# K ahead of q in the load queue, shifted copies behind the keys' copy, and the third w1 in halves of the model dimension

## The chip, the cores and the metric

The kernel runs on one core of one Trainium2 chip. The metric is the device time of one execution in microseconds, as the median of the runs shown. Times inside an execution are counted in microseconds from the start of its profiled span.

## What is computed

Sliding-window causal attention over 8 elements, 8 heads, 576 positions and a head dimension of 64, with a window of 64, followed by a mixture of experts in which a whole element goes to one expert: the mean over positions picks it.

```python
scores = scale * np.matmul(q, k.transpose(0, 1, 3, 2))
mask = (rel >= 0) & (rel < 64)
attn = softmax(np.where(mask, scores, -1e9))
x = matmul(attn, v)            # heads side by side: (8, 576, 512)
...
logits = x.mean(axis=1) @ w_gate                 # 8 experts
e_idx = np.argmax(logits, axis=1)
h = np.maximum(x[mask] @ w1[e], 0.0)             # 512 -> 1024
out[mask] = gate_w[mask, None, None] * (h @ w2[e])   # 1024 -> 512
```

## The kernel before

The attention is cut into 16 units, two for each element: unit u holds four heads of element u // 2. In the tables that a reader sees in the trace, a unit does the following.

- Two DMAs on POOL's queue bring its q and its K from float32 in memory to bfloat16 in SBUF (`load_qk`, tiles `qn` and `kn`, L211 and L214), q first.
- TensorE transposes K and q (`transpose_qk`, 18 small matmuls each, L334, tile `tp`), and a copy on DVE or ACT takes each from PSUM to SBUF (`leave_qk`, tile `dst`, L347, L301, L303).
- The scores come in three blocks (`scores_mm`, L380, tile `sp`). For each, ACT takes the Exp (`scores_out`, L398, tile `pt`) and DVE multiplies with a 0/1 mask (`mask_out`, L405).
- The values are multiplied in two halves of 20 matmuls (`values`, L426, tile `op`); the last third of each half reads the third block of `pt`. DVE divides by the row sums (`norm`, L440 and L442). The values lie in SBUF twice: `va`, cast from float32 by DVE (`cast_part` "whole", L303), and `vb`, the same shifted by 64 rows, which two copies make ("low" and "high", L303, from `va` to `vb`).

After two units an element's x is transposed (`transpose_x`, L463 on PE and L471 on ACT), the gate is computed (`gate`, L507 to L522), and the number of the chosen expert is read into a register of POOL, which then issues the loads of its weights: w1 (`load_w1`, L557 or L561) and w2 (`load_w2`, L567). They go through POOL's one queue, in the order of the program, with the loads of q and K. The expert's work is a stream of chunks (`expert_chunks`): eight chunks of the up projection, 8 matmuls each (`expert_up`, L599, tile `php`, followed by a Relu on ACT at L605 into `hT`), and five of the down projection (`expert_down`, L626 and L635, tile `pso`, followed by a copy into `ob` on DVE or ACT and a DMA on SP's queue).

The main loop runs in steps, from t = 4 on, one per unit. In step t stand the three score blocks and the two value halves of unit t, the transposes of unit t + 1, K's ahead of the first value half and q's between the halves, and `experts(pace)`, which is called eight times in most steps and puts chunks of an earlier element between the parts until an account of units of work is used up. An even step also holds the gate of element t // 2 - 1. The order of the code is the order on each engine (`P` keeps it). Step 6 holds the gate of element 2, the third one, so its chunks run from step 7 on.

PSUM has four buffers (pool `psum`), given out in turn, so a matmul that starts a new tile waits until the tile four places before has been read by ACT or DVE.

Weights come in two forms. For elements 0 to 2, w1 is loaded in pieces of the hidden dimension (`PARTS`; for element 2 two pieces of 512 columns, 512 KB each in SBUF), with the 128 columns of x that meet it side by side; each of the four rows of a piece in a partition is 1 KB long in SBUF. From element 3 on it comes in halves of the model dimension, also 512 KB each, in which a partition's part is one row of 4 KB, and x's columns are then taken with a stride of 2. A chunk needs one piece, but both halves. Elements 3 and 7 start with a pair of chunks (`expert_pair`), which takes the first half for two chunks and then the second half for both:

```python
for kbs in ((0, 1), (2, 3)):
    for f in (ft, ft + 1):
        expert_up(b, f, kbs)
```

Of the kernel before, what the change touches and what calls it, by code (L numbers as in the profile page):

```python
# [156 lines left out]
def kernel(  # L157
# [10 lines left out]
    nc = tc.nc  # L168
    B, H, S, D = q.shape
# [4 lines left out]
    FB = F // 128  # L174
# [5 lines left out]
    def P(ins):  # L180
        tc.keep_in_program_order(ins)
        return ins
# [16 lines left out]
    qv = q.rearrange("b h s d -> (b h s d)").rearrange(  # L199
        "(u s r c) -> u r s c", u=NU, s=2, c=NT * D)  # L200
# [7 lines left out]
    def load_qk(u):  # L208
        qn = qkn.tile([128, 2, NT * D], BF16, tag="qn")
        kn = qkn.tile([128, 2, NT * D], BF16, tag="kn")  # L210
        P(nc.gpsimd.dma_start(out=qn, in_=qv[u]))  # L211
        if u == 0:
            load_v(0)
        P(nc.gpsimd.dma_start(out=kn, in_=kv[u]))  # L214
        qk_tiles[u] = (qn, kn)

    v_tiles = {}

    def load_v(b, behind=None):
        vn = vpool.tile([128, NM, D], FP32, tag="vn")  # L220
        if behind is None:

            P(nc.gpsimd.memset(vn[:, 0, 0:1], 0.0))
        else:

            P(nc.gpsimd.tensor_copy(out=vn[:, 0, 0:1], in_=behind))
        v_tiles[b] = vn
        P(nc.sync.dma_start(out=vn, in_=vv[b]))
# [8 lines left out]
    wg = const.tile([128, KB, E], FP32)  # L237
    P(nc.scalar.dma_start(out=wg.rearrange("p (g kl) e -> p g kl e", kl=2), in_=moe_w_gate.rearrange("(g p kl) e -> p g kl e", p=128, kl=2)))

    wg0 = const.tile([128, KB, E], FP32)  # L240
# [25 lines left out]
    for (half, e, own) in ((0, 0, True), (1, 0, False), (0, 1, False), (1, 1, True)):  # L266
        sl = par[64 * half:64 * half + 64, e, :]
        if own:

            P(nc.gpsimd.affine_select(  # L270
                out=sl, in_=sl, compare_op=ALU.is_ge, fill=OUT, base=0,
                pattern=[[1, 64]], channel_multiplier=-1))
        else:

            P(nc.gpsimd.affine_select(
                out=sl, in_=sl, compare_op=ALU.is_ge, fill=OUT, base=-1,
                pattern=[[-1, 64]], channel_multiplier=1))
    outside = const.tile([128, 3, 6, 64], BF16)
    for c in range(3):
        P(nc.vector.tensor_copy(  # L280
            out=outside[:, c].rearrange("p (g e) w -> p g e w", e=2),
# [165 lines left out]

    def x_chunk(b, kb):

        if b < 3:  # L450
            return slice(128 * kb, 128 * kb + 128)
        return slice(256 * (kb // 2) + kb % 2, 256 * (kb // 2 + 1), 2)

# [31 lines left out]

    def gate_parts(b, kb):

        rows = wg0 if b < 3 else wg
        if kb == 0:
            gparts[b] = small.tile([128, E], FP32, tag="gpart", name=f"gpart{b}")  # L490
            P(nc.vector.tensor_scalar(
                out=gparts[b], in0=rows[:, kb, :], scalar1=pooled[:, b, kb:kb + 1],
                scalar2=None, op0=ALU.mult))
        else:
            P(nc.vector.scalar_tensor_tensor(  # L495
                out=gparts[b], in0=rows[:, kb, :], scalar=pooled[:, b, kb:kb + 1],
                in1=gparts[b], op0=ALU.mult, op1=ALU.add))
# [34 lines left out]
    def gate_weight(b):  # L532
# [8 lines left out]


    PARTS = (((0, 256), (256, 256), (512, 512)),
             ((0, 512), (512, 512)),
             ((0, 512), (512, 512)))

    def w1_part(b, i):
# [2 lines left out]
            :, KB * lo:KB * (lo + n)].rearrange("p (k f) -> p k f", k=KB)  # L550

    def load_w1(b):
        if b < 3:

            src = w1c[experts_of[b]].squeeze(0)
            for i, (lo, n) in enumerate(PARTS[b]):
                P(nc.gpsimd.dma_start(out=w1_part(b, i), in_=src[:, :, lo:lo + n]))  # L557
        else:

            for g in range(KB // 2):  # L560
                P(nc.gpsimd.dma_start(  # L561
                    out=weights[b][0][:, 2 * g:2 * g + 2, :],
                    in_=w1e[experts_of[b]].squeeze(0)[:, g]))
# [17 lines left out]
    def expert_up(b, ft, kbs=(0, 1, 2, 3)):  # L581
        if b == 0:
            part = min(ft // 2, 2)
            at = 256 * (ft // 2) - PARTS[b][part][0]
            w1t, cols = w1_part(b, part), slice(at + ft % 2, at + 256, 2)
        elif b < 3:
            w1t, cols = w1_part(b, ft // 4), slice(ft % 4, 512, 4)
        else:
            w1t, cols = weights[b][0], slice(512 * (ft // 4) + ft % 4, 512 * (ft // 4 + 1), 4)
        xT = xt_tiles[b]  # L590
        if ft == 0:
            h_tiles[b] = hpool.tile([128, FB, S], FP16, tag="hT", name=f"hT{b}")
        hT = h_tiles[b]
        if kbs[0] == 0:
            up_ps[b, ft] = psum.tile([128, 2, 512], FP32, tag="ps", name="php")
        php = up_ps[b, ft]
        for kb in kbs:
            for sc in range(2):
                P(nc.tensor.matmul(  # L599
                    out=php[:, sc, 0:288], lhsT=w1t[:, kb, cols],  # L600
                    rhs=xT[:, kb, ts(sc, 288)],
                    start=(kb == 0), stop=(kb == KB - 1)))
        if kbs[-1] < KB - 1:
            return
        P(nc.scalar.activation(  # L605
            out=hT[:, ft].rearrange("p (sc s) -> p sc s", sc=2),
            in_=php[:, :, 0:288], func=AF.Relu, scale=gatew[:, b:b + 1]))
# [63 lines left out]

    def expert_chunks():
        for b in range(B):
            if b in (3, B - 1):

                yield (lambda b=b: expert_pair(b, 0)), 2.0, nc.vector
            for ft in range(2 if b in (3, B - 1) else 0, FB):
                yield (lambda b=b, ft=ft: expert_up(b, ft)), 1.0, nc.vector
            left = [0, 1, 2, 3]
            tail[0] = True  # L680
            while left:

                if tail[0] and (halves[0] or len(left) == (3 if b == B - 1 else 1)):
                    tail[0] = False
                    yield (lambda b=b: expert_down(b, 4)), 0.9, nc.scalar
                else:
                    mt = left.pop(0)
                    yield (lambda b=b, mt=mt: expert_down(b, mt)), 1.7, nc.scalar
# [134 lines left out]
    for t in range(START + 1, NU + LAG):  # L823
        pace = per_step / 8.0 * 0.96
        on, prev, ahead = t < NU, START + 1 < t <= NU, t + 1 < NU

        def next_gate():
            b = t // 2 - 1
            gate(b, sp_ps[t, 2] if easy and on else None)
            load_w1(b)  # L830
            if START + 5 < t < NU - 3:
                load_qk(t + 3)
            load_w2(b)
            if t in (START + 3, START + 5):
                load_qk(t + 3)
            if t // 2 + 2 < B:
                load_v(t // 2 + 2)
            if t == START + 1:
                load_qk(7)

        gated = START < t <= NU and t % 2 == 0


        easy = gated and t > START + 3
        if t % 2 == 1 and t + 3 < NU:
            load_qk(t + 3)
        if prev:
            transpose_x(t - 1)
        if ahead and t > 5 and not gated:
            cast_part(t + 1, "whole")  # L850
        if on:
            scores(t, 0, easy or not gated)
            scores(t, 1, easy or not gated)
        if t > START + 1:
            experts(pace)
        if easy:
            experts(pace)
            if on:
                scores_mm(t, 2)
        if gated:  # L860

            next_gate()
            if on and not easy:
                mask_out(t, 0)
                mask_out(t, 1)
        if t == START + 1:
            experts(pace)
        if t == NU:
            gate_weight(B - 1)
            okc = row_check()  # L870
        if ahead and t > 5:
            if gated:
                cast_part(t + 1, "whole")
        if not easy:
            experts(pace)
        if on:
            if not easy:
                scores_mm(t, 2)
            scores_out(t, 2)
        if gated and on:  # L880
            gate_weight(t // 2 - 1)
        shifted = ahead and t > 5
        if shifted and not easy:
            cast_part(t + 1, "low")
            cast_part(t + 1, "high")
        if t == START + 1:
            cast_v(t)
        experts(pace)
        if shifted and easy:

            cast_part(t + 1, "low")
            cast_part(t + 1, "high")
        experts(pace)

        if ahead:
            transpose_qk(t + 1, 1, leave=False)
            leave_qk(t + 1, 1, free[0])

        late = t == START + 1
        if late:  # L900
            transpose_qk(t + 1, 0)
        elif on:
            values(t, 0)
        halves[0] = on
        experts(pace)
        experts(pace)
        if ahead and not late:
            transpose_qk(t + 1, 0)
        if late:
            values(t, 0)  # L910
        if on:
            values(t, 1)
        halves[0] = on
        if t == START + 2:
            cast_v(t + 1)
        if t == NU:
            row_flag(okc)
        experts(pace)
        experts(pace)
        if late:  # L920

            cast_v(t + 1)
# [38 lines left out]
```

## Time and profile before

| what | value |
|---|---|
| median of three runs | 216.69 us (215.91 to 217.36) |
| the profiled execution | 216.99 us |
| its span, first to last instruction | 215.1 us |
| TensorE busy | 200.3 us, 93% of the span |
| ACT, DVE busy | 134.8 us, 126.2 us |
| DMA | 45.64 MB moved, 212 GB/s in the mean |

Engines are named as in the profile: PE is TensorE's matmuls, PEld its weight loads, DVE VectorE, ACT ScalarE, POOL GpSimd and SP SyncE. A row of the timeline gives the start, the length, the engine, the line, the operation with its output and inputs, shapes, a count, and in brackets the idle time of the engine before it and what ended it. "DMA to landing" is the time from a DMA's issue until all of it has arrived. The three runs were not profiled; the profiled execution's own time is the one to set beside its span.

### The profile page before, as it was taken

The page shows a single profiled execution, that of the slowest core. Times are in us where ns is not written, and L with a number is a line of the kernel's source. Part 1 is how long each engine was busy: PE and PEld are TensorE (multiplying, and loading weights), DVE is VectorE, ACT ScalarE, POOL GpSimd, SP SyncE. Part 2 cuts the span into 40 slices and gives each one's busy share as a digit, 9 for nine tenths or more (in the row PEclk, how much of TensorE's full clock was granted, in tenths as well). Part 3 has the DMA queues.
Part 4 walks back from the last instruction along what each step waited for, and adds up shares of the span by engine and source line. Part 5 has one row for each costly group of instructions (what it writes and reads, how often), then busy time and mean ns, then how long its engine had stood idle before and what let it go on. Part 6 is the DMA issues. An engine that isn't in the chain of part 4 may idle for free.

```text
span 215.1 us, 7028 instructions
## 1 busy us (share of the span) xinstructions
PE 200.3 (93%) x3026; PEld 140.8 (65%) x3026; DVE 126.2 (59%) x307; ACT 134.8 (63%) x223; POOL 42.6 (20%) x75
## 2 busy tenths in 40 slices
PE   7777879999999998989999999999999999999991
PEld 2444657856687567856688567866688558748750
DVE  2536697656966967575673849394948763431030
ACT  2269597875479665885669566977489266714611
POOL 7180083035000630017000530032002100300000
PEclk9969999999999999999999999999999999999999
DMA  4999999999999999999999999999992997199533
GB/s 45 236 252 247 216 113 195 241 244 250 240 227 242 290 246 240 235 263 268 224 234 248 266 206 248 227 300 244 247 240 52 182 213 222 8 192 247 170 122 108
DMA packets 32485, 45.64 MB, mean 212 GB/s; under 512 B 2624, under 2 KB 24896, under 8 KB 32448
## 3 DMA queue, kind: packets, MB, share of 16 engines
q0 software_dynamic: 16272, 26.22, 68.2%
q1 hardware_dynamic: 15232, 18.75, 28.2%
q8 instruction: 25, 0.41, 0.7%
q10 hardware_dynamic: 944, 0.16, 0.4%
q14 instruction: 12, 0.10, 0.1%
HBM read 61.90 MB, written 9.44 MB: 332 GB/s over the span
## 4 chain that ended last, share of the span: by engine, by line
PE 67%; DMA 14%; ACT 7%; DVE 5%; issue 2%; POOL 2%; POOLq 0%
PE php L599 25%; PE pso L626 21%; DMA kn<-in_k_dram 10%; PE tp L334 6%; DMA qn<-in_q_dram 4%; PE op L426 4%; ACT xT L471 3%; PE sp L380 3%; PE pso L635 3%; PE tp L463 2%; ACT pt L398 2%; ACT hT L605 1%; DVE vb L303 1%; PE idle L714 1%; DVE va L303 1%
## 5 line engine op out<-in xcount | busy, mean ns | idle before, releaser
L599 PE MATMUL php<-xT,w1t 128*128 128x288 f16 x512 | 69.6, 287 | 1.5 <-ACT pt L398 0.9
L605 ACT ACTIVATE hT<-php,gatew 128x576 f16<-128x576 f32 x64 | 46.8, 751 | 26.6 <-PE php L599 26.5
L599 PEld LDWEIGHTS <-w1t 128*128 128x128 f16 x512 | 55.0, 113 | 9.1 <-DMA w1t<-in_moe_w_dram 1.0
L626 PE MATMUL pso<-w2t,hT 128*128 128x512 f16 x248 | 58.6, 380 | 0.3 <-DVE ob L303 0.3
L398 ACT ACTIVATE pt<-sp 128x768 f16<-128x768 f32 x48 | 36.7, 822 | 6.4 <-PE sp L380 6.4
L626 PEld LDWEIGHTS <-hT 128*128 128x128 f16 x248 | 22.6, 99 | 25.4 <-issue 1.4
L303 DVE COPY ob<-pso 128x512 f32<-128x512 f32 x23 | 15.8, 688 | 21.5 <-PE pso L626 21.4
L405 DVE TENSOR_TENSOR pt<-pt,masks 128x768 f16<-128x768 f16 x42 | 23.0, 556 | 7.0 <-ACT pt L398 6.0
L442 DVE TENSOR_TENSOR x<-op,linv 128x640 f16<-128x640 f32 x32 | 26.4, 824 | 1.1
L561 POOL DMA_DIRECT2D w1t<-in_moe_w_dram x10 | 6.0, 601 | 94.5 <-PE tp L334 19.6
L347 ACT COPY dst<-tp 128x1152 bf16<-128x1152 bf16 x16 | 18.0, 1123 | 9.5 <-PE tp L334 9.2
L471 ACT ACTIVATE xT<-tp 128x576 f16<-128x576 f16 x28 | 17.9, 647 | 8.8 <-PE tp L463 8.8
L426 PE MATMUL op<-vb,pt 128*64 128x65 f16 x320 | 15.8, 195 | 1.1 <-ACT pt L398 0.6
L303 DVE COPY vb<-va 64x1152 f16<-64x1152 f16 (+1 forms) x32 | 15.2, 476 | 2.2 <-ACT va L301 1.7
L426 PEld LDWEIGHTS <-pt 128*64 128x64 f16 x640 | 13.5, 111 | 3.8 <-issue 2.4
L380 PE MATMUL sp<-dst 64*64 64x128 bf16 (+1 forms) x672 | 14.0, 213 | 2.0 <-ACT dst L301 0.8
L426 PE MATMUL op<-va,pt 128*64 128x65 f16 x320 | 15.6, 195 | 0.0
L495 DVE SCALAR_TENSOR_TENSOR gpart<-wg,pooled,gpart 128x8 f32<-128x8 f32 x21 | 4.8, 227 | 18.3 <-ACT xT L471 18.0
L380 PEld LDWEIGHTS <-dst 64*64 64x64 bf16 x672 | 10.0, 107 | 8.3 <-issue 4.5
L557 POOL DMA_DIRECT2D w1t<-in_moe_w_dram x7 | 5.5, 793 | 43.0 <-PE sp L380 20.3
L303 DVE CAST va<-vn 128x1152 f16<-128x1152 f32 x15 | 11.3, 755 | 4.5 <-DMA vn<-in_v_dram 4.5
L301 ACT COPY ob<-pso 128x512 f32<-128x512 f32 x8 | 4.7, 586 | 14.2 <-PE pso L626 14.2
(85 smaller groups left out, 197.1 us busy)
## 6 DMA issues: line engine op xcount, KB each, us to landing
w2t<-in_moe_w_dram POOLq DMA_DIRECT2D x8, 1024.0 KB, 16.3
out_dram<-ob SPq DMA_DIRECT2D x31, 256.0 KB, 7.7
w1t<-in_moe_w_dram POOLq DMA_DIRECT2D x15, 512.0 KB, 8.6
qn<-in_q_dram POOLq DMA_DIRECT2D x16, 288.0 KB, 15.8
kn<-in_k_dram POOLq DMA_DIRECT2D x16, 288.0 KB, 17.4
out_dram<-ob SPq DMA_DIRECT2D x16, 64.0 KB, 7.5
w1t<-in_moe_w_dram POOLq DMA_DIRECT2D x2, 256.0 KB, 4.9
vn<-in_v_dram SPq DMA_DIRECT2D x8, 0.2 KB, 19.1
```

Source lines behind the costliest of these rows:

```text
L303: P(eng.tensor_copy(out=out, in_=in_))
L334: P(nc.tensor.transpose(out=tp[64 * s:64 * s + 64, ts(t, 128)], in_=src[:, s, ts(t, D)], identity=ident, tile_position=(0, 64 * s)))
L347: P(nc.scalar.copy(out=dst.rearrange("p (x r t) -> p x r t", x=2, t=NT), in_=view))
L380: P(nc.tensor.matmul(out=sp[64 * half:64 * half + 64, s, 64 * (qblk - 6 * c):64 * (qblk - 6 * c) + n], lhsT=kT[64 * s:64 * s + 64, ts(kblk ...
L398: P(nc.scalar.activation(out=pt, in_=sp[:, :, 0:384], func=AF.Exp, scale=scale))
L405: P(nc.vector.tensor_tensor(out=pt, in0=pt, in1=masks[:, c].rearrange("p s g w -> p s (g w)"), op=ALU.mult))
L426: P(nc.tensor.matmul(out=op[64 * half:64 * half + 64, xx, 65 * jj:65 * jj + 65], lhsT=pt[:, s, 64 * (g % 6):64 * (g % 6) + 64], rhs=win, s ...
L442: P(nc.vector.tensor_tensor(out=x[:, :, h0 * D:(h0 + 2) * D].rearrange("p j (x c) -> p x j c", x=2), in0=view[:, :, :, 0:64], in1=li[:, :, ...
L471: P(nc.scalar.activation(out=xT[:, kb, :], in_=tp[:, kl, 0:S], func=AF.Copy, accum_out=pooled[:, b, kb:kb + 1]))
L599: P(nc.tensor.matmul(out=php[:, sc, 0:288], lhsT=w1t[:, kb, cols], rhs=xT[:, kb, ts(sc, 288)], start=(kb == 0), stop=(kb == KB - 1)))
L605: P(nc.scalar.activation(out=hT[:, ft].rearrange("p (sc s) -> p sc s", sc=2), in_=php[:, :, 0:288], func=AF.Relu, scale=gatew[:, b:b + 1]))
L626: P(nc.tensor.matmul(out=pso[:, 0, :], lhsT=hT[:, fb, ts(mt, 128)], rhs=w2t[:, fb, :], start=(fb == 0), stop=(fb == FB - 1)))
```

## The change

It has three parts. From unit 6 on, `load_qk` issues K's load ahead of q's. In the even steps from 8 on, the two shifted copies of the next unit's values (`low` and `high`) stand behind the copy of the next unit's keys, and so behind one more call of `experts`. Element 2 takes its w1 in two halves of the model dimension, with the strided columns of x and the gate rows that go with them, and begins with a pair of chunks, as elements 3 and 7 do.

```diff
@@ load_qk
-        P(nc.gpsimd.dma_start(out=qn, in_=qv[u]))
-        if u == 0:
-            load_v(0)
+        if u < 6:
+            P(nc.gpsimd.dma_start(out=qn, in_=qv[u]))
+            if u == 0:
+                load_v(0)
         P(nc.gpsimd.dma_start(out=kn, in_=kv[u]))
+        if u >= 6:
+
+            P(nc.gpsimd.dma_start(out=qn, in_=qv[u]))
@@ x_chunk
-        if b < 3:
+        if b < 2:
             return slice(128 * kb, 128 * kb + 128)
@@ gate_parts
-        rows = wg0 if b < 3 else wg
+        rows = wg0 if b < 2 else wg
@@ PARTS
     PARTS = (((0, 256), (256, 256), (512, 512)),
-             ((0, 512), (512, 512)),
              ((0, 512), (512, 512)))
@@ load_w1
-        if b < 3:
+        if b < 2:
@@ expert_up
-        elif b < 3:
+        elif b < 2:
@@ expert_chunks
-            if b in (3, B - 1):
+            if b in (2, 3, B - 1):
                 yield (lambda b=b: expert_pair(b, 0)), 2.0, nc.vector
-            for ft in range(2 if b in (3, B - 1) else 0, FB):
+            for ft in range(2 if b in (2, 3, B - 1) else 0, FB):
@@ the main loop
         experts(pace)
-        if shifted and easy:
-
-            cast_part(t + 1, "low")
-            cast_part(t + 1, "high")
         experts(pace)
         if ahead:
             transpose_qk(t + 1, 1, leave=False)
             leave_qk(t + 1, 1, free[0])
+        if shifted and easy:
+
+            cast_part(t + 1, "low")
+            cast_part(t + 1, "high")
```

What this makes of the order on the engines is shown at three places. In the rows, numbers behind names are buffers; `hT_1848` and `hT_1859` are the hidden activations of element 2, `w1t_1593` and `w2t_1594` its weights.

On ACT in step 7, from the Exp of the first two score blocks of unit 7 on, before:

```order
L398 ACTIVATE pt<-sp 128x768 x2
L605 ACTIVATE hT_1848<-php,gatew 128x576
L398 ACTIVATE pt<-sp 128x768
L605 ACTIVATE hT_1848<-php,gatew 128x576 x3
L347 COPY dst<-tp 128x1152
```

and after the change:

```order
L402 ACTIVATE pt<-sp 128x768 x2
L608 ACTIVATE hT_1859<-php,gatew 128x576 x2
L402 ACTIVATE pt<-sp 128x768
L608 ACTIVATE hT_1859<-php,gatew 128x576 x2
L351 COPY dst<-tp 128x1152
```

The Exp of the third score block has moved behind the second Relu, as that block's 14 matmuls have moved behind the second chunk on PE.

On DVE in step 10, from the mask of the third score block of unit 10 on, before:

```order
L405 TENSOR_TENSOR pt<-pt,masks 128x768
L538 RECIPROCAL gatew<-gsum 128x1
L303 COPY vb_123<-va_121 64x18x64 x2
L303 COPY ob<-pso 128x512
L440 RECIPROCAL linv<-op 128x10
```

and after the change:

```order
L409 TENSOR_TENSOR pt<-pt,masks 128x768
L542 RECIPROCAL gatew<-gsum 128x1
L307 COPY ob<-pso 128x512
L307 COPY vb_123<-va_121 64x18x64 x2
L444 RECIPROCAL linv<-op 128x10
```

The two shifted copies and the output copy have changed places. In step 12 it is the same; in step 14 it is K's copy with which they change places, and in step 8 nothing stands between, so the order there is as before.

On POOL in steps 6 and 7, with the weights of element 2 and the loads of units 9 and 10, before:

```order
L557 DMA w1t_1593<-in_moe_w_dram 128x4x512
...
L567 DMA w2t_1594<-in_moe_w_dram 128x2x2048
L211 DMA qn<-in_q_dram 128x2x576
L214 DMA kn<-in_k_dram 128x2x576
L223 MEMSET vn 128x1
L211 DMA qn<-in_q_dram 128x2x576
L214 DMA kn<-in_k_dram 128x2x576
```

and after the change:

```order
L564 DMA w1t_1593<-in_moe_w_dram 128x2048
...
L570 DMA w2t_1594<-in_moe_w_dram 128x2x2048
L215 DMA kn<-in_k_dram 128x2x576
L218 DMA qn<-in_q_dram 128x2x576
L227 MEMSET vn 128x1
L215 DMA kn<-in_k_dram 128x2x576
L218 DMA qn<-in_q_dram 128x2x576
```

Each load of w1 (there are two, one is left out) has one long row in a partition instead of four, and K and q have changed places.

## The prediction

> **What bounds the kernel now.** I read the page first, then PE's waits, then the timelines of the four places where the diff acts, then the DMA landings behind them. The page gives the span, TensorE's share, its busy slices, the busy slices of the DMA engines, and the two queues.
>
> ```profile
> span 215.1 us, 7028 instructions
> PE 200.3 (93%) x3026; PEld 140.8 (65%) x3026; DVE 126.2 (59%) x307; ACT 134.8 (63%) x223; POOL 42.6 (20%) x75
> PE   7777879999999998989999999999999999999991
> DMA  4999999999999999999999999999992997199533
> q0 software_dynamic: 16272, 26.22, 68.2%
> q1 hardware_dynamic: 15232, 18.75, 28.2%
> ```
>
> TensorE is busy nearly everywhere, and the DMA engines are too until about 160 us. So PE's order sets the end, and a load that is a little late shows as a hole in PE. After the first 50 us the holes are few. These rows of the waits hold those that the change can touch (waiting line, releaser, us in total, times, longest).
>
> ```profile
> PE tp L334 <- DMA kn<-in_k_dram: 1.2, 2, 0.8
> PE php L599 <- ACT pt L398: 0.9, 2, 0.6
> PEld L599 <- DMA w1t<-in_moe_w_dram: 1.0, 1, 1.0
> PE pso L626 <- DVE ob L303: 0.3, 1, 0.3
> ```
>
> PE's timeline at the three places (start, length, line, idle time before it in brackets):
>
> ```profile
> 79.00 1.90 PE L626 MATMUL pso<-w2t,hT 128*128 128x512 f16 x8
> 81.45 1.17 PE L599 MATMUL php<-xT,w1t 128*128 128x288 f16 x8 [0.55 <-ACT pt L398]
> 82.56 0.36 PE L380 MATMUL sp<-dst 64*64 64x64 bf16 x14
> 82.85 1.17 PE L599 MATMUL php<-xT,w1t 128*128 128x288 f16 x8
> 83.95 0.69 PE L334 MATMUL tp<-ident,kn 128*64 128x128 bf16 x18
> 85.00 2.15 PE L599 MATMUL php<-xT,w1t 128*128 128x288 f16 x16
> ...
> 96.57 0.69 PE L334 MATMUL tp<-ident,kn 128*64 128x128 bf16 x18 [0.81 <-DMA kn<-in_k_dram]
> ...
> 122.01 1.89 PE L626 MATMUL pso<-w2t,hT 128*128 128x512 f16 x8 [0.27 <-DVE ob L303]
> ```
>
> The three holes sum to 0.55 + 0.81 + 0.27 = 1.63 us. PE's instructions do not change in number or size, so 1.63 us (0.75% of the span) is all that the change can win by taking waits away.
>
> **The change part by part.** First the DMA side of w1 of element 2: issues, landings counted from the issue (of two: first, mean, second), the chain's wait for the K of unit 9, and w1 and w2 of elements 3 and 6 for comparison.
>
> ```profile
> 50.82 0.72 POOL L214 DMA_DIRECT2D kn<-in_k_dram  x1
> kn<-in_k_dram POOLq DMA_DIRECT2D x1, 288.0 KB, 25.6
> ...
> L557 POOL DMA_DIRECT2D w1t<-in_moe_w_dram x2: 750/754/757, 71.8 to 72.6; - x2
> DMA to landing us min/median/max: 9.6/11.4/13.1
> 73.32 0.72 POOL L567 DMA_DIRECT2D w2t<-in_moe_w_dram  x1
> w2t<-in_moe_w_dram POOLq DMA_DIRECT2D x1, 1024.0 KB, 18.2
> 74.01 0.74 POOL L211 DMA_DIRECT2D qn<-in_q_dram  x1
> qn<-in_q_dram POOLq DMA_DIRECT2D x1, 288.0 KB, 19.8
> 74.73 21.80 DMA kn<-in_k_dram
> ...
> L561 POOL DMA_DIRECT2D w1t<-in_moe_w_dram x2: 566/610/653, 96.1 to 96.7; - x2
> DMA to landing us min/median/max: 8.0/9.1/10.3
> ...
> L561 POOL DMA_DIRECT2D w1t<-in_moe_w_dram x2: 563/622/681, 165.3 to 166.0; - x2
> DMA to landing us min/median/max: 5.2/7.0/8.7
> ```
>
> The K of unit 8, last in the queue ahead of w1, lands at 50.82 + 25.6 = 76.4. The two pieces of w1 land at 71.8 + 9.6 = 81.4 and 72.6 + 13.1 = 85.7: 1024 KB in 9.3 us. The 1024 KB of w2 behind them land at 73.3 + 18.2 = 91.5, in 5.8 us. Element 3's w1, in halves of the model dimension, has its halves at 104.1 and 107.0, 2.9 us apart, which is w2's pace. So I take 2.9 us a half: the first lands at 79.3, the second at 82.2. The ends: it cannot matter before PE asks for it (81.95, below); the widest spacing of halves is element 6's, 166.0 + 8.7 - (165.3 + 5.2) = 4.2 us, and two of those give 84.8. I take 82.2 because w2 is the nearest row, the same engines right behind, and element 3 agrees.
>
> What it removes: PE is free at 80.90 and now waits 0.55 for the first piece; the first half is 1.6 us early, so this hole goes.
>
> What it moves: the pair puts two chunks' matmuls (8 and 8) ahead of the last score block of unit 7, which stood between them. A chunk takes 1.10 us on PE (81.45 to 82.56), so the second half is asked for at 80.90 + 1.05 = 81.95 and comes at 82.2, a new wait of 0.25. The chunks finish together, late, and ACT runs both Relus before the Exp of the last score block. ACT and DVE there now (Relu, Exp, Relu; then the mask, the shifted copies, K's copy):
>
> ```profile
> 82.66 0.74 ACT L605 ACTIVATE hT<-php,gatew 128x576 f16<-128x576 f32 x1 [1.25 <-PE php L599]
> 83.30 0.80 ACT L398 ACTIVATE pt<-sp 128x768 f16<-128x768 f32 x1
> 84.06 0.74 ACT L605 ACTIVATE hT<-php,gatew 128x576 f16<-128x576 f32 x1
> ...
> 84.14 0.56 DVE L405 TENSOR_TENSOR pt<-pt,masks 128x768 f16<-128x768 f16 x1 [1.53 <-ACT pt L398]
> 84.61 0.92 DVE L303 COPY vb<-va 64x1152 f16<-64x1152 f16 x2
> 85.56 1.36 DVE L303 COPY dst<-tp 128x1152 bf16<-128x1152 bf16 x1
> ```
>
> Now the chain runs: first Relu 0.10 after its chunk's last matmul, next ACT instruction 0.64 later, mask 0.84 after Exp's start (83.30 to 84.14), PE's next chunk 0.86 after the mask's start (84.14 to 85.00), because the last third of the value matmuls reads the masked block. With the second half at 82.2: first chunk done at 82.75, Relu 82.85, second Relu 83.49, Exp 84.13, mask 84.97, next chunk on PE at 85.83 instead of 85.00. So this place costs +0.83 net: hole gone, pair in, mask late. In general that chunk starts 3.63 us after the second half lands. The lower end is no wait for it, 81.95 + 3.63 = 85.58, +0.58; with 84.8 it is 88.43, +3.43. Behind the late mask on DVE stand the shifted copies, K's copy (waited for by q's transposes) and the normalisation; all move by the same amount as PE, so nothing is paid twice.
>
> K ahead of q: unit 9's q lands at 74.0 + 19.8 = 93.8, its K at 74.73 + 21.80 = 96.5, and PE asks for K at 95.76. With K first it has q's place, 2.0 us ahead of need: -0.81. The halves alone would do it too (9.3 - 5.8 = 3.5 us earlier: 93.0), so the two edits earn this once. The price is q's: its transposes come behind K's, 20 value matmuls and two chunks. Unit 9's q in K's place (96.5) is asked for at 100.2 and is in time:
>
> ```profile
> 100.22 0.69 PE L334 MATMUL tp<-ident,qn 128*64 128x128 bf16 x18
> ```
>
> For units 6 to 8 and 10 to 15 no row shows a wait for K, so q in K's place has more room than K had: 0.
>
> Shifted copies behind K's copy: in step 10 DVE runs them ahead of an output copy for which PE waits.
>
> ```profile
> 120.33 0.90 DVE L303 COPY vb<-va 64x1152 f16<-64x1152 f16 x2
> 121.26 0.69 DVE L303 COPY ob<-pso 128x512 f32<-128x512 f32 x1
> ```
>
> The output copy then starts at 120.4 and ends near 121.1, before PE is free at 121.74: -0.27. The output's transfer on SP's queue starts 0.9 us earlier. The copies are for the next unit's values, a step later, so their 0.9 us stays covered. Steps 12 and 14 swap likewise, with no hole in PE there: 0. The lower end is -0.27; if the next wait (the normalisation, which now stands behind the same copies, unmoved) takes its place, 0. I take -0.27. The strided columns of x and the other gate rows of element 2 keep shapes and counts, and so do the instructions issued for them: 0, since nothing is added. On POOL an issue of a half takes 610 ns against 754 for a piece, so w2 and what is behind it in POOL's row are issued 0.3 us earlier, into a queue that is busy until 76.4: 0.
>
> Sum: +0.83 - 0.81 - 0.27 = -0.25 us. The profiled execution took 216.99 us with a span of 215.1, and the median of the three runs is 216.69, 0.30 below it. So the median goes to 216.69 - 0.25 = 216.4 us.
>
> **Rivals.** (1) Slower: the second half comes late. At element 6's spacing (84.8) the sum is +3.43 - 0.81 - 0.27 = +2.35, 219.0 us; if halves move no faster than the pieces do (85.7), the place costs 85.7 + 3.63 - 85.00 = +4.33 and the sum is +3.25, 219.9 us. Over 1% (2.17 us) it is from a landing of 84.6 on. For it: w1's queue shares the engines with output and V traffic. Against it: 5.8 us for w2 beside such traffic. The Trainium skill (DMA: Bandwidth & Descriptors, Specifications) puts line rate at transfers of 512 B or more; both forms are above it (1 KB and 4 KB a row in SBUF), so by that rule the halves win nothing and 219.9 us follows. The trace does not agree: 9.3 us against 5.8 us for 1024 KB.
> (2) Faster: the holes go and nothing takes their place, -1.63, 215.1 us. The order on ACT speaks against it: Exp stands behind two Relus, and DVE had been waiting 1.53 us for that Exp.
> (3) The swap of K and q does nothing because the halves already bring K early. It gives the same 216.4; a run with one edit alone would tell.
>
> **How the numbers follow.** Chances: the forecast with the second half landing before 83.3 (a sum of -0.5 to +0.85) 0.66; rival 2, or part of it, 0.16; rival 1 0.18, of which 0.15 is over 1% (0.06 of it halves no faster than pieces). Rival 3 lies within the first. About 1% is what a measurement of this kernel can tell from no change: the three runs alone span 215.91 to 217.36. Rival 2's 215.1 is within 1%, and only with a lucky run does it pass 214.5: faster 0.05. Within 1%: 0.80. Slower: 0.15. The range starts below rival 2 by a little (214.9) and reaches 218.6, which takes in landings up to 84.3; it leaves out most of rival 1.
>
> **What would show it.** In the profile after: no PE hole ahead of the first chunk of element 2, the second half landing near 82.2, a PE hole of about 1.2 us inside unit 7's value matmuls released by DVE's mask, no wait for K of unit 9, no hole before the second down-projection of step 10. If PE runs unit 7's values without a hole, my ACT chain is wrong; if the second half lands at 84 or later, my pace is.

## The result, and the profile after

| | before | changed |
|---|---|---|
| median, us (22 runs of each) | 216.22 (215.02 to 218.65) | 217.19 (216.17 to 218.78) |
| profiled execution, us | 216.99 | 217.21 |
| its span, us | 215.1 | 215.3 |

The ratio of changed to before is 1.0055, with a 95% interval of 1.0037 to 1.0074: slower by about 1.2 us, clear of noise though under 1%. The forecast was 216.4 us, 0.25 us faster than before. The measured 217.19 lies within the forecast's range, but the sign is wrong.

The page of the changed kernel (span, busy time of the engines, PE's and the DMA engines' slices, the two busy queues):

```profile
span 215.3 us, 7022 instructions
PE 199.1 (92%) x3023; PEld 140.2 (65%) x3026; DVE 127.0 (59%) x307; ACT 134.8 (63%) x223; POOL 42.6 (20%) x75
...
PE   7777879999999996999999999998999999999991
...
DMA  5999999999999999999999999999991997199633
...
q0 software_dynamic: 15504, 26.22, 68.5%
q1 hardware_dynamic: 15232, 18.75, 28.1%
```

The work is the same and as dense as before; only the packets of q0 are fewer (15504 for 16272) for the same bytes, which is the longer row of w1. The difference has to be sought in single holes. PE's waits in the changed kernel (waiting line, releaser, us in total, times, longest) now name other releasers than before (of the two waits for w1, the second, 0.55, is at 31.5 us, in the start-up):

```profile
PE php L602 <- DMA w1t<-in_moe_w_dram: 1.4, 2, 0.9
PE op L430 <- DVE pt L409: 1.1, 1, 1.1
...
PE pso L629 <- DVE x L446: 0.6, 1, 0.6
```

PE's timeline in the changed kernel at the same places as in the prediction, and at a fourth, in step 12 (the last row):

```profile
78.73 1.67 PE L629 MATMUL pso<-w2t,hT 128*128 128x512 f16 x7
80.25 1.14 PE L602 MATMUL php<-xT,w1t 128*128 128x288 f16 x8
82.27 1.17 PE L602 MATMUL php<-xT,w1t 128*128 128x288 f16 x8 [0.88 <-DMA w1t<-in_moe_w_dram]
83.37 0.36 PE L384 MATMUL sp<-dst 64*64 64x64 bf16 x14
83.66 0.69 PE L338 MATMUL tp<-ident,kn 128*64 128x128 bf16 x18
...
85.70 0.22 PE L430 MATMUL op<-vb,pt 128*64 128x65 f16 x1 [1.13 <-DVE pt L409]
...
85.95 2.15 PE L602 MATMUL php<-xT,w1t 128*128 128x288 f16 x16
...
96.64 0.69 PE L338 MATMUL tp<-ident,kn 128*64 128x128 bf16 x18
...
121.75 1.90 PE L629 MATMUL pso<-w2t,hT 128*128 128x512 f16 x8
...
146.88 1.90 PE L629 MATMUL pso<-w2t,hT 128*128 128x512 f16 x8 [0.56 <-DVE x L446]
```

The three holes of before (0.55, 0.81, 0.27; 1.63 together) are all gone. In their place stand 0.88 inside the pair, 1.13 inside unit 7's value matmuls and 0.56 in step 12: 2.57 together. The difference, +0.94, is nearly that of the medians, 217.19 - 216.22 = +0.97. The two spans differ by only 0.2, mainly because PE came to step 7 half a microsecond earlier in this execution (free at 78.73 + 1.67 = 80.40, against 80.90; the first row is the end of a group that began ahead of the window). That comes from the start-up, which the change does not touch: the gate's product of element 1 already stood at 43.36 us, against 44.13.

ACT and DVE of the changed kernel behind the pair (both Relus, the Exp of the last score block, the mask):

```profile
82.98 1.37 ACT L608 ACTIVATE hT<-php,gatew 128x576 f16<-128x576 f32 x2 [2.06 <-PE php L602]
84.25 0.81 ACT L402 ACTIVATE pt<-sp 128x768 f16<-128x768 f32 x1
```

```profile
85.09 0.56 DVE L409 TENSOR_TENSOR pt<-pt,masks 128x768 f16<-128x768 f16 x1 [2.98 <-ACT pt L402]
```

DVE waited 2.98 us for that Exp, where it had waited 1.53. The DMA issues of the changed kernel: the last load of unit 8 (now q), the two halves of element 2's w1, and unit 9's K (below each, the time from issue to landing, smallest, middle, largest):

```profile
L218 POOL DMA_DIRECT2D qn<-in_q_dram x1: 723/723/723, 50.4 to 50.4; - x1
...
DMA to landing us min/median/max: 25.3/25.3/25.3
...
L564 POOL DMA_DIRECT2D w1t<-in_moe_w_dram x2: 541/564/588, 71.2 to 71.8; - x2
...
DMA to landing us min/median/max: 8.1/9.3/10.4
...
L215 POOL DMA_DIRECT2D kn<-in_k_dram x1: 728/728/728, 73.1 to 73.1; - x1
...
DMA to landing us min/median/max: 18.0/18.0/18.0
```

Unit 8's last load landed at 50.4 + 25.3 = 75.7, the halves at 71.2 + 8.1 = 79.3 and 71.8 + 10.4 = 82.2, unit 9's K at 91.1, over 5 us before PE asks for it at 96.6. The second half's clock time, 82.2, is the one forecast, but by luck: it is 6.5 us behind the load ahead of it, not 5.8, and PE was there half a microsecond sooner.

The place that the prediction put at nothing is step 12. DVE before (the shifted copies, the output copy, the normalisation):

```profile
143.16 0.96 DVE L303 COPY vb<-va 64x1152 f16<-64x1152 f16 x2
144.15 0.69 DVE L303 COPY ob<-pso 128x512 f32<-128x512 f32 x1
...
145.17 0.82 DVE L442 TENSOR_TENSOR x<-op,linv 128x640 f16<-128x640 f32 x1
```

and DVE after:

```profile
143.72 0.69 DVE L307 COPY ob<-pso 128x512 f32<-128x512 f32 x1 [0.73 <-PE pso L629]
144.33 1.38 DVE L307 COPY vb<-va 64x1152 f16<-64x1152 f16 x2
...
146.00 0.82 DVE L446 TENSOR_TENSOR x<-op,linv 128x640 f16<-128x640 f32 x1
```

Before, the copies ran while DVE would have waited for the output's matmuls. After, DVE stands idle there for 0.73 us, the copies come behind the output copy, and they take 1.38 instead of 0.96. The normalisation behind them starts at 146.00 instead of 145.17, and PE's second down-projection waits 0.56 for it, where before (146.50) it had not waited.

### The profile page after: what moved, and what is told of

Read it like the earlier page. It is cut to its first block, busy times and chain, and to the rows that moved or that the text cites. A ratio compares the mean times of both kernels' runs of the same rounds, so it can differ in the third digit from the quotient of the medians.

```text
span 215.3 us, 7022 instructions
## 1 busy us (share of the span) xinstructions
PE 199.1 (92%) x3023; PEld 140.2 (65%) x3026; DVE 127.0 (59%) x307; ACT 134.8 (63%) x223; POOL 42.6 (20%) x75
## 3 DMA queue, kind: packets, MB, share of 16 engines
q0 software_dynamic: 15504, 26.22, 68.5%
## 4 chain that ended last, share of the span: by engine, by line
PE 72%; DMA 11%; ACT 7%; DVE 5%; issue 2%; POOLq 1%; POOL 0%; another core or an unknown queue 0%
PE php L602 29%; PE pso L629 22%; DMA w1t<-in_moe_w_dram 7%; PE tp L338 6%; PE op L430 4%; DMA kn<-in_k_dram 3%; PE sp L384 3%; PE tp L467 3%; PE pso L638 3%; ACT pt L402 2%; ACT xT L475 2%; ACT hT L608 2%; DVE x L446 1%; PE idle L717 1%; DVE ob L307 1%
## 5 line engine op out<-in xcount | busy, mean ns | idle before, releaser
L564 POOL DMA_DIRECT2D w1t<-in_moe_w_dram x12 | 7.0, 581 | 115.8 <-PE pso L629 41.0
L307 DVE COPY vb<-va 64x1152 f16<-64x1152 f16 (+1 forms) x32 | 16.0, 501 | 0.9 <-ACT va L305 0.4
L307 DVE COPY dst<-tp 128x1152 bf16<-128x1152 bf16 x8 | 10.8, 1356 | 3.2 <-PE tp L338 3.1
```

The costliest lines, as they stand in the source:

```text
L307: P(eng.tensor_copy(out=out, in_=in_))
```

## The experiments

Theory A: the loss is made in step 7. The second half lands while PE stands in the pair, and everything behind the pair (second Relu, Exp, mask, the rest of the values, the next chunk) is late by as much. The rivals: the order alone does it, whatever the form of the load; the late half alone does it, whatever the order; it comes from K and q or from the copies in step 12. The ratios below are to the kernel before, run on the same chip, with 95% intervals; the two medians follow, the experiment's first.

**K ahead of q alone**, in the kernel before. The edit is the change's own in `load_qk`, for the units from 6 on, and nothing else.

> K ahead of q from unit 6 on, alone. Theory A (the changed kernel is slower because the pair of chunks and the moved copies open new holes in PE; K first is a gain): the hole of 0.81 us ahead of the K transposes of unit 9 is gone and no other appears, 0.4% faster where the kernel before has that hole. Rival (K first is empty, because K is not late in most executions): ratio 1.000, and the profile of this kernel would have no such hole either way.

Ratio 1.0023 (0.9995 to 1.005), 216.76 and 216.42 us. PE's timeline of this kernel at the first piece of w1, at unit 9's K, and further on:

```profile
81.35 0.93 PE L603 MATMUL php<-xT,w1t 128*128 128x288 f16 x6 [0.74 <-DMA w1t<-in_moe_w_dram]
...
95.58 0.69 PE L338 MATMUL tp<-ident,kn 128*64 128x128 bf16 x18
...
130.19 0.68 PE L603 MATMUL php<-xT,w1t 128*128 128x288 f16 x4 [0.40 <-DMA w1t<-in_moe_w_dram]
```

The wait for K is gone, as forecast, and no time is won: the 0.4% that I had expected lies outside the interval. In this execution PE waits longer for the first piece (0.74) and elsewhere for a later w1 (0.40).

**The halves and the pair alone**, in the kernel before (the bounds `b < 3` become `b < 2` wherever the change has them):

```diff
-             ((0, 512), (512, 512)),
              ((0, 512), (512, 512)))
...
-            if b in (3, B - 1):
+            if b in (2, 3, B - 1):
                 yield (lambda b=b: expert_pair(b, 0)), 2.0, nc.vector
-            for ft in range(2 if b in (3, B - 1) else 0, FB):
+            for ft in range(2 if b in (2, 3, B - 1) else 0, FB):
```

> Third w1 in halves with the pair of chunks, alone. Theory A: in unit 7 a hole of 0.3 to 0.9 us inside the pair (second half late) and one of 1.1 us inside the value matmuls (mask late), the hole of 0.55 ahead of the first chunk gone: +0.9 to +1.5 us at this place; the K of unit 9 comes 3 us earlier even behind q, so no hole there; in sum +0.1 to +0.7 us, or up to +1.5 where the kernel before has no K hole. Rival (all the loss is the moved copies): no hole in unit 7's values, ratio under 1.000.

Ratio 1.007 (1.0043 to 1.0097), 217.58 and 216.42 us, at the upper end of what I expected: the whole loss is in this part. Its PE timeline shows the same two holes:

```profile
83.51 1.17 PE L598 MATMUL php<-xT,w1t 128*128 128x288 f16 x8 [1.07 <-DMA w1t<-in_moe_w_dram]
...
86.95 0.22 PE L426 MATMUL op<-vb,pt 128*64 128x65 f16 x1 [1.14 <-DVE pt L405]
```

There is no wait for unit 9's K in it either, though K is still behind q: it lands at 93.9 and is asked for at 97.9. So the swap of K and q does nothing that the halves do not do, which is the prediction's third rival.

**The copies behind K's copy alone**, in steps 8, 10, 12 and 14:

```diff
-        if shifted and easy:
-            cast_part(t + 1, "low")
-            cast_part(t + 1, "high")
         experts(pace)
         if ahead:
             transpose_qk(t + 1, 1, leave=False)
             leave_qk(t + 1, 1, free[0])
+        if shifted and easy:
+            cast_part(t + 1, "low")
+            cast_part(t + 1, "high")
```

> Shifted copies behind K's copy, alone. Theory A: the hole of 0.27 us in step 10 is gone, one of 0.3 to 0.6 us appears in step 12 ahead of the second down-projection chunk (released by the normalisation on DVE), sum 0.0 to +0.3 us. Rival (my prediction's term): -0.27 us and no hole in step 12.

Ratio 1.0005 (0.9979 to 1.0032), 216.41 and 216.42 us. The hole in step 10 is gone, and step 12 has the new one, as in the changed kernel:

```profile
145.95 1.90 PE L626 MATMUL pso<-w2t,hT 128*128 128x512 f16 x8 [0.62 <-DVE x L442]
```

0.27 won and 0.62 lost is within the interval; the time alone would not tell it, the timeline does.

**The changed kernel with the score block first.** In step 7 the third score block and its Exp go ahead of the pair:

```diff
-        if not easy:
+        if not easy and t != 7:
             experts(pace)
...
             scores_out(t, 2)
+        if t == 7:
+            experts(pace)
```

> The changed kernel with one more edit: in step 7 the third score block and its Exp stand ahead of the pair, as in step 9. Theory A (late mask through the order on ACT): the hole of 1.1 us inside unit 7's value matmuls is gone, the wait for the second half stays at about 0.5 us; 1.4 us faster than the changed kernel, about 0.2% faster than the kernel before. Rival (the late second half alone holds everything up): the value matmuls still wait, and the time stays within 0.5 us of the changed kernel.

Ratio 0.9986 (0.9952 to 1.002), 215.96 and 216.42 us. Against the changed kernel's 1.0055 that is 0.0069, or 1.5 us, and the two intervals do not meet. Its PE timeline (score block, pair, K's transposes, third chunk):

```profile
81.57 0.36 PE L384 MATMUL sp<-dst 64*64 64x64 bf16 x14
81.86 2.41 PE L602 MATMUL php<-xT,w1t 128*128 128x288 f16 x16
84.20 0.69 PE L338 MATMUL tp<-ident,kn 128*64 128x128 bf16 x18
...
85.15 1.05 PE L602 MATMUL php<-xT,w1t 128*128 128x288 f16 x7
```

No hole stands ahead of the values: the mask no longer hangs on the landing. Only what stands between the landing and the third chunk was changed, and by the ratio the loss is gone. That is what Theory A says. Of the wait for the second half, 0.5 us expected, little is left in this execution (the pair takes 2.41 us for 2.15), since PE comes to it at 81.86; in the run with the copies moved in step 10 only, below, the wait is there.

In step 12, where this kernel has the changed kernel's order, PE waits only 0.09 us, since the two copies take 0.91 us here and not 1.38:

```profile
143.54 0.91 DVE L307 COPY vb<-va 64x1152 f16<-64x1152 f16 x2
```

**The order alone**: the kernel before, with its two pieces, but element 2's first two chunks together ahead of the third score block:

```diff
-            for ft in range(2 if b in (3, B - 1) else 0, FB):
+            if b == 2:
+                yield (lambda b=b: [expert_up(b, f) for f in (0, 1)]), 2.0, nc.vector
+            for ft in range(2 if b in (2, 3, B - 1) else 0, FB):
```

> The kernel before, with its two pieces of w1, but the first two chunks of element 2 next to each other ahead of the third score block of unit 7. Only the order of the change, none of its loads. Theory A (the late mask comes from the order): a hole of about 1.1 us inside unit 7's value matmuls, released by DVE's mask; about +1.1 us, ratio 1.003 to 1.006. Rival (it comes from the late second half): no such hole, within 0.2 us of the kernel before.

Ratio 1.0015 (0.9987 to 1.0042), 216.06 and 216.18 us, smaller than I expected. PE's timeline of it:

```profile
79.95 2.15 PE L599 MATMUL php<-xT,w1t 128*128 128x288 f16 x16
...
84.22 0.22 PE L426 MATMUL op<-vb,pt 128*64 128x65 f16 x1 [0.99 <-DVE pt L405]
```

The hole at the mask comes without any half and without a wait for w1, so the order makes it. What it costs in time stays unclear: the interval, -0.3 to +0.9 us, holds 0 and the +0.4 of the holes (0.99 come, 0.55 gone), but not the +1.1 that I expected.

**The whole change but for the pair**: the third w1 in halves, its chunks one by one:

```diff
-            if b in (2, 3, B - 1):
+            if b in (3, B - 1):
                 yield (lambda b=b: expert_pair(b, 0)), 2.0, nc.vector
-            for ft in range(2 if b in (2, 3, B - 1) else 0, FB):
+            for ft in range(2 if b in (3, B - 1) else 0, FB):
```

> The whole change, but element 2's first two chunks as single chunks, with the third score block between them. Theory A: no hole in unit 7's value matmuls; the first chunk waits in its middle for the second half, 0.8 to 1.4 us; about 0.6 to 1.0 us faster than the changed kernel, ratio to the kernel before 0.999 to 1.003. Rival (late second half alone makes the loss): as slow as the changed kernel, 1.005.

Ratio 1.0045 (1.0019 to 1.0072), 216.91 and 216.18 us: a miss, I had expected 0.999 to 1.003. Its PE timeline (the work ahead, the second part of the first chunk, the third chunk):

```profile
79.43 1.90 PE L629 MATMUL pso<-w2t,hT 128*128 128x512 f16 x8
...
83.64 0.68 PE L602 MATMUL php<-xT,w1t 128*128 128x288 f16 x4 [1.82 <-DMA w1t<-in_moe_w_dram]
...
86.69 2.15 PE L602 MATMUL php<-xT,w1t 128*128 128x288 f16 x16
```

A chunk alone needs both halves. It has four matmuls of the first half to run, not eight, and then waits for the second; the mask hole is gone, but the wait is 1.82. From PE being free (79.43 + 1.90 = 81.33) to the third chunk it is 5.36 us here, against 4.10 before and 5.55 in the changed kernel. So a late second half costs nearly as much without the pair, since the third score block stands behind the wait here too, and Theory A, as I had put it, gave too much to the order. (0.51 of this kernel's waits is that of step 12, as in the changed kernel.)

**Score block first, copies moved in step 10 only.** The edit of the score block, and the copies stay in their old place in every step but 10 (`t not in (10,)` at the old place, `t in (10,)` at the new one):

> The changed kernel with the third score block of step 7 ahead of the pair, and the shifted copies behind K's copy in step 10 alone. Theory A: no hole over 0.3 us after step 5 except what DMA luck makes; 0.1 to 0.5 us faster than the run with the block first alone, ratio to the kernel before 0.995 to 0.999. Rival (the remaining holes are DMA luck in both): no faster than the run with the block first.

Ratio 0.9986 (0.9958 to 1.0015), 215.46 and 216.18 us: by its ratio no better than with the copies moved in all steps, as its rival says. PE's timeline of its pair, with the wait back but nothing behind it:

```profile
82.30 1.17 PE L602 MATMUL php<-xT,w1t 128*128 128x288 f16 x8 [0.91 <-DMA w1t<-in_moe_w_dram]
```

**The kernel before, profiled a second time:**

> A second look at the kernel before. Theory A (the hole ahead of unit 9's K is chance in the landings of one execution): K lands about when PE asks for it, the hole differs by several tenths from 0.81 us or is absent. Rival (it is a fixed cost): 0.7 to 0.9 us at the same place.

217.0 us in this one execution. PE's timeline at unit 9's K and at a later w1:

```profile
95.59 0.69 PE L334 MATMUL tp<-ident,kn 128*64 128x128 bf16 x18 [0.20 <-DMA kn<-in_k_dram]
...
153.87 0.68 PE L599 MATMUL php<-xT,w1t 128*128 128x288 f16 x4 [0.92 <-DMA w1t<-in_moe_w_dram]
```

The same program: K's wait is 0.20 here, not 0.81, and a wait of 0.92 for a w1 at 153.87 is there that the first execution did not have.

**The pieces kept, the rest done well**: the kernel before, with K first, the score block first in step 7 and the copies moved in step 10 only.

> The kernel before with its two pieces of w1; K ahead of q, the third score block of step 7 ahead of element 2's first chunk, and the shifted copies behind K's copy in step 10 alone. Theory A (what counts in step 7 is what stands between a landing and the next chunk): the third chunk starts 3.1 to 3.3 us after the first piece lands, not 3.6; holes of steps 8 and 10 gone; 0.3 to 1.0 us faster than the kernel before, ratio 0.995 to 0.999. Rival (the halves are needed for a gain): no faster than the kernel before, 1.000.

Ratio 1.0015 (0.9985 to 1.0045), 216.54 and 215.97 us; I had expected 0.995 to 0.999, and the rival's 1.000 is within the interval. The third chunk starts 3.9 us after the first piece lands, not 3.1 to 3.3, because PE itself comes to the first chunk 0.9 us after the landing, so that this expectation was not tested. All three holes of before are gone, and PE's timeline has another, at element 3's w1:

```profile
106.64 1.17 PE L603 MATMUL php<-xT,w1t 128*128 128x288 f16 x8 [0.81 <-DMA w1t<-in_moe_w_dram]
```

With the pieces, then, these edits show no gain in time, while in the changed kernel the score block first is worth 1.5 us.

**The copies moved in step 12 alone**, in the kernel before (`t not in (12,)` at the old place, `t in (12,)` at the new one):

> Shifted copies behind K's copy in step 12 alone. Theory A: the hole of step 10 (0.26 us) stays, one of 0.1 to 0.6 us appears in step 12 ahead of the second down-projection chunk, released by the normalisation: 0.1 us if the two copies take 0.45 us each, 0.6 us if they take 0.7 each under POOL's issues; +0.1 to +0.6 us. Rival (the hole of step 12 was made by something else in the change): no hole there.

Ratio 1.0001 (0.9971 to 1.0031), 216.2 and 215.97 us. A hole appears at the place, 0.33 us smaller than in the changed kernel, as the copies were 0.33 us less slowed (1.05 us, not 1.38). PE's timeline and DVE's:

```profile
146.00 1.90 PE L626 MATMUL pso<-w2t,hT 128*128 128x512 f16 x8 [0.23 <-DVE x L442]
```

```profile
143.78 1.05 DVE L303 COPY vb<-va 64x1152 f16<-64x1152 f16 x2
```

**The changed kernel with the copies moved in step 10 only** (the same edit as above, with 10):

> The changed kernel with the shifted copies behind K's copy in step 10 alone. Theory A: no hole in step 12; the two holes of unit 7 stay (0.9 and 1.1 us); 0.3 to 0.6 us faster than the changed kernel, ratio to the kernel before 1.003. Rival (step 12 costs nothing in the end): as slow as the changed kernel, 1.0055.

Ratio 1.0035 (1.0009 to 1.006), 216.9 and 215.97 us. The step 12 hole is gone and step 7 is as in the changed kernel (a wait of 1.17 in the pair and 1.13 at the mask). It is where I expected it, 0.002 or 0.4 us under the changed kernel, but the two intervals overlap, so the time does not show it by itself.

**Step 7 in all traces.** The time from PE being free, at the end of the down-projection ahead of element 2's first two chunks, to the third chunk. The matmuls in between are the same ones in all of them, in different orders:

| kernels | us |
|---|---|
| two pieces, order as before (five executions) | 3.35 to 4.29, 3.95 on average |
| two pieces, the order alone | 4.60 |
| halves, without the pair | 5.36 |
| halves and pair, order as in the change (three) | 5.55, 5.74, 5.83 |
| halves and pair, score block first (two) | 3.51, 4.35 |
| two pieces, score block first | 3.25 |

In these traces the order alone adds 0.65 us to the average of before, the late half alone 1.4, both together 1.6 to 1.9. With the score block ahead of the wait even a late half (4.35, with its wait of 0.91) costs 0.4.

## Why the prediction was wrong

Two terms make the wrong sign: the pace of the first half (0.62 us too little) and step 12, which was put at nothing (0.56). A third, K's wait, was too large a credit. Step by step, against the sum of +0.83 - 0.81 - 0.27 = -0.25:

- **The chain behind the pair** was right. The prediction's rule was that the third chunk starts 3.63 us after the second half lands. It started 85.95 - 82.2 = 3.75 after it (3.73 in the two other kernels in this order), and the hole inside the values, 1.2 us forecast, was 1.13, 1.14 and 1.13 in the three kernels with halves and pair in this order. The order alone makes such a hole (0.99), and the score block moved ahead of the pair removes it. Rival 2, with nothing in the holes' place, fell on this, as argued.
- **"So I take 2.9 us a half"** is the step that failed, by its size: the first half, right behind the load ahead, did not come at that pace. From unit 8's last load to the second half I forecast 5.8 us. Measured: 6.5 in the changed kernel, and between 6.4 and 7.2 in the five experiments with halves. In the changed kernel the first half took 79.3 - 75.7 = 3.6 and the second 2.9; in all six traces with halves the first took 3.4 to 4.2 and the second 2.7 to 3.2. Why the first takes longer stays open. In its 3.6 us the queue moved 0.68 MB, more than the 0.52 MB of a half, so some of the 16 engines were already at what stands behind it. So the pair waits 0.88 (1.07 and 1.17 in the two other kernels in this order), not 0.25. From PE being free to the third chunk went 85.00 - 80.90 = 4.10 us before and 85.95 - 80.40 = 5.55 after. The place costs +1.45, not +0.83, and the difference, 0.62, is the longer wait in the pair (0.63). It is rival 1's mechanism, with a smaller delay than its row of element 6 gave.
- **"With K first it has q's place, 2.0 us ahead of need: -0.81"** was right for the execution that I read and wrong as a credit. With q first, and PE not held up ahead, K's wait was 0.81, 0.20, 0.56 and 0 in four executions (the kernel before twice, the copies of step 12 alone, the copies alone), 0.39 on average. The profiled execution was itself 0.77 above the median of 22 runs. The edit alone wins nothing that can be measured.
- **The halves bring K early too** was right: the halves alone have no wait for K.
- **Step 10, -0.27** was right: the hole goes wherever the copies move there, and nothing takes its place.
- **"Steps 12 and 14 swap likewise, with no hole in PE there: 0"** failed in step 12. It looked at PE's holes before and not at who would stand behind the copies. The copies had filled DVE's wait for the output's matmuls; moved behind the output copy they delay the normalisation, and PE waits 0.56 for it. In the five traces with this order in step 12, PE's wait is the time of the two copies less 0.82 us: 0.62, 0.56, 0.51, 0.23 and 0.09 us for copies of 1.45, 1.38, 1.33, 1.05 and 0.91. So with copies as fast as the prediction's rows have them (0.90 and 0.92) the new order costs 0.1 us; the rest is that they are slower at the new place in four of the five.

With what was measured the sum is +1.45 - 0.81 - 0.27 + 0.56 = +0.93 against the execution profiled before, and +1.35 with K's mean wait of 0.39 for its 0.81. The medians say +0.97, and the ratio with its interval +0.8 to +1.6. Both fit. With averages for step 7 too (5.71 - 3.95 = +1.76) it is +1.66, just above the interval, so the close agreement of the first sum is in part the choice of the execution.

What stays open: the parts do not add up in time as they do in holes. K first alone, and the pieces with all three holes removed, were not faster; in both, and in the second execution of the kernel before, some other w1 landed late (0.40, 0.81, 0.92). It fits with DMA engines that are busy until about 160 us, so that PE, earlier at one place, waits at the next; but that is argued, not shown. Single executions cannot settle it: the gate's product of element 1, ahead of all that any edit here touches, stands at 42.9 to 44.6 us in the 13 traces, a spread as large as the holes. No version was shown to beat the kernel before: the two with halves and the score block first have 0.9986 each, with intervals that reach over 1. Both of them beat the changed kernel. Nor are the halves shown to be worth anything there: with the rest the same, pieces have 1.0015 and halves 0.9986, and the intervals overlap.

## What to carry to other kernels

Judge a load that lands about when it is needed by what stands between its landing and the work that follows it: put work that doesn't need the load ahead of the wait, so that one late landing is not paid again by the chain behind it. Before a wait's removal is credited, look at the same wait in a second execution, since waits of half a microsecond for a DMA came and went here in the same program. Where a step is moved to let something pass, name what stands behind its new place, not only what stood behind the old one.

## What the runs showed of the hardware

DVE's shifted copies (64x1152 or 64x1088, f16) take 0.44 to 0.46 us when POOL issues nothing beside them (232 in all 13 traces). Beside POOL's issues of w1 alone they take 0.43 to 0.53 (69). Beside its issues of q, K or w2 they take up to 0.74, and 41 of 115 took over 0.55. The copies of step 12, at 144.33 us in the changed kernel and at 143.16 before, came from beside issues of w1 to beside issues of K and q, here POOL's timeline of the changed kernel:

```profile
143.99 0.71 POOL L215 DMA_DIRECT2D kn<-in_k_dram  x1
144.69 0.74 POOL L218 DMA_DIRECT2D qn<-in_q_dram  x1
```

The Trainium skill (SBUF — State Buffer, the section on the two separate sides) says that DVE in some modes and GpSimd share a pair of ports under a lock, which whoever starts first holds for its whole instruction. The traces agree only in part: the copies were lengthened, but by 0.30 us at most, beside issues of 0.7 us, and 74 of the 115 stayed under 0.55. Why some are slowed and others not these runs don't show: with the score block first, the copies of step 12 took 0.91 us beside the same two issues.

1024 KB of w1 in halves took 6.4 to 7.2 us from the landing of the load ahead of it, in two pieces of the old form 8.6 to 9.4. The form was worth 2.3 us on the whole load, comparing the averages (6.7 and 9.0), as forecast in kind. In the packet records a packet of 1 KB takes 97 ns of an engine (the kernel before) and one of 4 KB 323 ns (the changed kernel). By an estimate from these two figures, 1024 KB are 6.2 us of all 16 engines in the one form and 5.2 in the other, which is 1.0 of the 2.3 us; the rest these runs don't explain. It still did not help, since the old form's first piece, all that the first chunks need, was there 4.3 to 5.1 us after that load, earlier than the second half.
